# A block-sparse attention and SoLU kernel: the first pass rearranged and the order of the last two tiles changed

## The chip, the core and the metric

The kernel runs on one core of a Trainium2 chip. The core has a matrix engine (TensorE, PE in the profile; its weight loads are listed as PEld), VectorE (DVE), ScalarE (ACT), GpSimd (POOL) and SyncE (SP, which here only issues transfers). Each engine works through its own instructions in order and waits on semaphores for the others. Data moves between main memory and the on-chip SBUF by DMA, issued from the queues of SP, ACT or POOL; TensorE writes to PSUM, which has eight banks, and VectorE and ScalarE read it. The metric is device time in microseconds: a median of several runs, and one further execution taken with the hardware profiler.

## What is computed

Four sequences of 768 tokens have eight heads of 64 columns. Attention is masked in blocks of 32 by 32: a query block sees its neighbours, the first and last block, three drawn blocks per row, and everything if it is itself first or last. The result, as 3072 rows of 512, passes through a feed-forward layer whose activation is h times softmax(h), then a layer norm and a second matrix:

```python
scores = scale * np.matmul(q, k.transpose(0, 1, 3, 2))
scores = np.where(mask, scores, -1000000000.0)
attn = softmax(scores)
x = (attn @ v).transpose(0, 2, 1, 3).reshape(3072, 512)
h = x @ w_in                      # 512 -> 1024
solu = h * softmax(h)
ln = (solu - mean) / np.sqrt(var + 1e-06) * g_ln
out = ln @ w_out                  # 1024 -> 512
```

## The kernel before

**Tiling.** Heads go in pairs (NPR = 4 pairs), a head in each half of the 128 partitions. Keys are cut into six tiles of 128; one unit takes a pair, two key tiles (j of NJ = 3) and 256 queries (r of PPB = 3). So UP = 12 units make a pass, three passes a batch, and 144 units the whole attention. Unit s has a score (`score`, L327: four matmuls, L335), an exponential by ScalarE of 128x1024 (L348), a mask, and eight matmuls with v (`outs`, L365, L375). After three units VectorE divides by the row sums (`normalise`, L381).

**Masks.** Most units are masked by VectorE, which multiplies the exponentials with a 0/1 tile from `mask_sb` (`mask`, L355). For units with j = 1 after the first three, `adds_mask` (L350) has TensorE add a large negative number instead, by four further matmuls with `hid` and `onehot` (L343). Seven mask tiles are needed; `make_mask` (L548) builds them, two to a PSUM tile, by matmuls from `vis_t` and `onehot` and a copy.

**Turning k and q.** Both need the head's columns on the partitions. For batch 0 they are loaded as fp32, cast to bf16 (`cast_st`, L299, on VectorE), turned by six TensorE transposes into PSUM and copied out (`turn_kq`, L307; k by ScalarE, q by VectorE). For the other batches GpSimd casts and SP issues transposing DMAs (`turn_dma`, L315). v is only cast (`cast_v`, L304): by ScalarE in batch 0, by GpSimd later.

**Setup.** VectorE and GpSimd build the block mask (`vis`, L503 to L540) from the drawn blocks `samp_i`, which are loaded first on SP's queue (L488). k and q of pair 0 are loaded by SP and ACT, the other raw tiles, g_ln and w_out by SP. `onehot` and `hid` are copied to partitions 64 to 127 by DMAs from ACT's queue (L566). w_in comes by a GpSimd DMA (L576). Eleven matmuls on zeros (`N_IDLE`, L498) run first on TensorE.

**The second layer.** Each pass gives two tiles of 128 rows (t = 0 to 23). A tile goes through: transposing DMA (`moe_x`), h (`moe_h`), exponential, solu on VectorE (`moe_u`), transposing DMA (`moe_t`), statistics (`moe_b`, bn_stats twice), the reciprocal deviation by Ln and Exp on ScalarE (`moe_r`), eight matmuls with w_out (`moe_o`, L443), and scaling and storing (`moe_y`, L453). The last two tiles, 22 and 23, take functions of their own (`tail_x`, `tail_h`, `tail_e`, `tail_u`, `tail_t`, `tail_b`, L632 to L681), which turn by TensorE instead of DMA and work in halves. `check_r`, `check_e` and `check_b` test the range of all sums; the result `bad_i` is read by every engine at the end and decides whether a general path runs (it does not here).

**Order.** The order on each engine is that of the program: the loop (L725) runs slots s = 0, 1, 2, ...; in a slot come score(s), outs of older units, normalise, mask(s - 2), and then whatever `at(slot, ...)` has put down for it. Slot 147 (`s0 = n_units + LAG`) is the first after attention. An engine starts an instruction when the ones ahead of it in its own order and the data it needs are done, so slots set order, not times. DMAs issued from SP and ACT take turns on eight semaphores, and one waits until the earlier DMA on its semaphore has landed.

**PSUM.** `p_s` has three tiles of two banks (scores, h, masks, transposes), `p_op` one bank (P·V, and some of the last outputs), `p_o` one bank (outputs of the second layer, the eleven first matmuls, the mean of w_out).

Of the kernel before, what the change touches and what calls it, by code (L numbers as in the profile page):

```python
# [7 lines left out]
FP32 = mybir.dt.float32  # L8
# [193 lines left out]
def kernel(  # L202
# [11 lines left out]
    nc = tc.nc  # L214
# [92 lines left out]
    def turn_kq(which, b, a, copy):  # L307
        st = staged.pop((which, b, a)).rearrange("p i h d -> p i (h d)")
        tp = p_s.tile([TQ, NT, TQ], BF16, tag="s", name=f"tp{which}{b}_{a}")
        for i in range(NT):  # L310
            nc.tensor.matmul(tp[:, i, :], st[:, i, :], ident, is_transpose=True,
                             start=(i == 0), stop=(i == NT - 1))
        copy(out=(kTs, qTs)[which][b][:, a, :], in_=tp.rearrange("p i x -> p (i x)"))  # L313
# [36 lines left out]
    def adds_mask(s):  # L350


        return s >= NJ and s % NJ == 1
# [99 lines left out]
    def moe_y(t):  # L453
        ot = mo.tile([128, d_model], FP32, tag="ot", name=f"ot{t}")
        if t < n_tail - 2:
# [25 lines left out]
    def centre_w(c):  # L481
# [6 lines left out]
    nc.sync.dma_start(out=samp_i.rearrange("a b c -> a (b c)"),  # L488
                      in_=bass.AP(tensor=_t32, offset=0, ap=[[2 * NR, NB], [1, 2 * NR]]))
# [3 lines left out]

    idle = setup.tile([128, 512], BF16, name="idle")
    nc.vector.memset(idle, 0.0)
    idle_ps = p_o.tile([128, 512], FP32, tag="o")
    for i in range(N_IDLE):
        nc.tensor.matmul(idle_ps, idle[:, 0:128], idle, start=True, stop=True)  # L498
    nc.vector.memset(ident, 0.0)
    nc.gpsimd.affine_select(out=ident, in_=ident, compare_op=ALU.not_equal, fill=1.0,  # L500
                            base=0, channel_multiplier=1, pattern=[[-1, 128]])

    vis = setup.tile([NB, NB], FP32, name="vis")  # L503
    nc.vector.memset(vis, 1.0)
    onehot = setup.tile([128, NT, TQ], BF16, name="onehot")
    nc.vector.memset(onehot[0:64], 1.0)
    kbi = setup.tile([NB, NB], I32, name="kbi")
    nc.gpsimd.iota(kbi, pattern=[[1, NB]], base=0, channel_multiplier=0)
    for fill, base, cm, step in (
        (0.0, 1, -1, 1), (0.0, 1, 1, -1),  # L510
        (1.0, -1, 1, 0), (1.0, NB - 2, -1, 0),
        (1.0, -1, 0, 1), (1.0, NB - 2, 0, -1),
    ):
        nc.gpsimd.affine_select(out=vis, in_=vis, compare_op=ALU.is_ge, fill=fill,
                                base=base, channel_multiplier=cm, pattern=[[step, NB]])

    for base, cm, sgn in ((0, -BLK, 1), (BLK - 1, BLK, -1)):
        nc.gpsimd.affine_select(out=onehot[0:64], in_=onehot[0:64], compare_op=ALU.is_ge, fill=0.0,
                                base=base, channel_multiplier=cm,
                                pattern=[[sgn, NT], [sgn * NT, TQ]])  # L520
# [6 lines left out]
    for i in range(2):  # L527
# [3 lines left out]
                "(c p) m -> p c m", p=128))  # L531
    kbf = setup.tile([NB, NB], FP32, name="kbf")
    nc.vector.tensor_copy(out=kbf, in_=kbi)
    samp_f = setup.tile([NB, NR], FP32, name="samp_f")
    nc.vector.tensor_copy(out=samp_f, in_=samp_i[:, :, 0])
    for i in range(NR):
        nc.vector.scalar_tensor_tensor(out=vis, in0=kbf, scalar=samp_f[:, i : i + 1], in1=vis,
                                       op0=ALU.is_equal, op1=ALU.max)
    vis_t = setup.tile([NB, NB, BLK], BF16, name="vis_t")
    nc.vector.tensor_copy(out=vis_t, in_=vis.rearrange("p (q o) -> p q o", o=1)  # L540
                          .broadcast_to([NB, NB, BLK]))
    vis_k = vis_t.rearrange("a n o -> a (n o)").rearrange("a (p i) -> a i p", i=NT)

    mask_at = [(0, 0), (0, 1), (0, 2)] + [(r, j) for r in range(1, PPB) for j in (0, NJ - 1)]
    mask_sb = setup.tile([TQ, len(mask_at), 512], BF16, name="mask_sb")
    n_mask = (len(mask_at) + 1) // 2

    def make_mask(n, copy):  # L548
        m = p_s.tile([TQ, 2, 512], FP32, tag="s", name=f"m{n}")
        lst = mask_at[2 * n : 2 * n + 2]  # L550
        for u, (r, j) in enumerate(lst):
            for i in range(2):
                nc.tensor.matmul(m[:, u, i * 256 : (i + 1) * 256], vis_k[:, 2 * j + i, :],  # L553
                                 onehot[0:NB, r * QW : (r + 1) * QW, :],
                                 start=(i == 0), stop=(i == 1), skip_group_check=True)
        copy(out=mask_sb[:, 2 * n : 2 * n + len(lst), :], in_=m[:, 0 : len(lst), :])


    hid = setup.tile([128, S], BF16, name="hid")
    nc.gpsimd.memset(hid[0:64], 0.0)  # L560
    hid_k = hid.rearrange("a (p i) -> a i p", i=NT)
# [10 lines left out]
    for vb in vbuf:  # L572
        nc.vector.memset(vb[:, :, :, :, D:D1], 1.0)
    nc.vector.memset(mean_w, 1.0 / d_ff)
    nc.vector.memset(ones_c, 1.0)
    nc.gpsimd.dma_start(out=w_in_sb, in_=moe_w_in.rearrange("(c p) f -> p c f", p=128))  # L576
# [205 lines left out]
```

## Time and profile before

| | |
|---|---|
| median of 3 runs | 241.1 us (241.05 to 241.48) |
| profiled execution | 240.45 us, of which the span of the core 238.9 us |
| mean granted TensorE clock | 0.954 |
| busy: PE, DVE, ACT, POOL | 211.5, 195.4, 182.4, 38.7 us |
| first score starts | 10.28 us |
| last matmul of the second layer ends | 229.16 us |
| last ScalarE instruction ends | 233.29 us |

The profile lists busy time, but an engine that is busy need not set the end. The chain of work goes back from the last instruction, step by step, to what released it. The waits say for each engine what ended its idle time. Windows give busy time and the granted clock of any stretch. Times are microseconds from the start of the span, and L with a number is a line of the kernel.

### The profile page before, as it was taken

The page shows a single profiled execution, that of the slowest core. Times are in us where ns is not written, and L with a number is a line of the kernel's source. Part 1 is how long each engine was busy: PE and PEld are TensorE (multiplying, and loading weights), DVE is VectorE, ACT ScalarE, POOL GpSimd, SP SyncE. Part 2 cuts the span into 40 slices and gives each one's busy share as a digit, 9 for nine tenths or more (in the row PEclk, how much of TensorE's full clock was granted, in tenths as well). Part 3 has the DMA queues.
Part 4 walks back from the last instruction along what each step waited for, and adds up shares of the span by engine and source line. Part 5 has one row for each costly group of instructions (what it writes and reads, how often), then busy time and mean ns, then how long its engine had stood idle before and what let it go on. Part 6 is the DMA issues. An engine that isn't in the chain of part 4 may idle for free.

```text
span 238.9 us, 6023 instructions
## 1 busy us (share of the span) xinstructions
PE 211.5 (89%) x2407; PEld 109.9 (46%) x2407; DVE 195.4 (82%) x417; ACT 182.4 (76%) x263; POOL 38.7 (16%) x53
## 2 busy tenths in 40 slices
PE   7588877869999999998999997999999999999930
PEld 2265553544545444453454544445454545454410
DVE  6587679799898978888899889689988988896480
ACT  2496897967987888797798887889888988883630
POOL 6300030413122132411202132312000000000000
PEclk9755899999999999999999999999999999999996
DMA  6999917699999999999878999998832514333211
GB/s 191 340 265 316 365 29 150 149 227 199 261 179 230 202 190 276 230 184 218 223 166 204 196 214 258 209 206 224 130 74 59 134 44 86 92 91 88 84 42 62
DMA packets 73765, 42.33 MB, mean 177 GB/s; under 512 B 56708, under 2 KB 69124, under 8 KB 73732
## 3 DMA queue, kind: packets, MB, share of 16 engines
q1 hardware_dynamic: 72772, 40.26, 73.4%
q0 software_dynamic: 528, 1.05, 2.3%
q10 hardware_dynamic: 432, 0.59, 0.8%
q8 instruction: 20, 0.33, 0.6%
q14 instruction: 13, 0.11, 0.2%
HBM read 23.07 MB, written 6.29 MB: 123 GB/s over the span
## 4 chain that ended last, share of the span: by engine, by line
PE 50%; DMA 19%; DVE 14%; ACT 5%; issue 5%; SPq 4%; POOL 1%; ACTq 0%; POOLq 0%
PE o L450 12%; PE s L335 11%; PE h L406 10%; PE op L375 10%; DMA lnT<-solu 9%; DMA raw<-in_k_dram 5%; DVE ex L360 4%; ACT ex L348 3%; DMA raw<-in_q_dram 3%; SPq L317 2%; PE s L343 2%; DVE stats L426 2%; DMA raw<-in_v_dram 2%; DVE w_out_sb L482 2%; PE h L649 2%
## 5 line engine op out<-in xcount | busy, mean ns | idle before, releaser
L348 ACT ACTIVATE ex<-s 128x1024 bf16<-128x1024 f32 x144 | 139.0, 1023 | 6.8 <-PE s L335 5.3
L360 DVE TENSOR_TENSOR ex<-ex,mask_sb 128x1024 bf16<-128x1024 bf16 x97 | 70.2, 724 | 8.0 <-ACT ex L348 7.9
L335 PE MATMUL s<-qT,kT 64*128 64x256 bf16 x576 | 57.5, 282 | 4.7 <-DVE qT L313 1.9
L375 PE MATMUL op<-v,ex 128*128 128x65 bf16 x1152 | 52.9, 196 | 5.7 <-DVE ex L360 3.5
L450 PE MATMUL o<-w_out_sb,lnT 128*128 128x512 bf16 x192 | 52.0, 381 | 4.1 <-DMA lnT<-solu 3.2
L375 PEld LDWEIGHTS <-ex 128*128 128x128 bf16 x1152 | 41.4, 99 | 26.0 <-issue 13.1
L410 ACT ACTIVATE e<-h 128x1024 bf16<-128x1024 f32 x22 | 22.5, 1024 | 25.0 <-PE h L406 25.0
L406 PE MATMUL h<-w_in_sb,xT 128*128 128x512 bf16 x176 | 41.6, 379 | 0.0
L335 PEld LDWEIGHTS <-kT 64*128 64x128 bf16 x576 | 19.4, 95 | 42.9 <-issue 36.9
L301 POOL CAST st<-raw 128x768 bf16<-128x768 f32 x24 | 21.9, 911 | 82.8 <-DMA raw<-in_k_dram 56.0
L426 DVE BATCH_NORM_STATS2 stats<-solu 128x6 f32<-128x512 bf16 x44 | 30.0, 684 | 0.0
L415 DVE TENSOR_TENSOR solu<-h,e 128x1024 bf16<-128x1024 f32 x22 | 26.8, 1217 | 0.0
L450 PEld LDWEIGHTS <-lnT 128*128 128x128 bf16 x192 | 14.0, 97 | 21.3 <-issue 8.0
L456 DVE TENSOR_SCALAR ot<-o,rstd 128x512 f32<-128x512 f32 x20 | 15.0, 750 | 10.3 <-PE o L450 10.2
L406 PEld LDWEIGHTS <-xT 128*128 128x128 bf16 x176 | 15.9, 98 | 16.0
L389 DVE TENSOR_TENSOR xb<-op,recip_all 128x256 bf16<-128x256 f32 x48 | 20.4, 424 | 1.6
L343 PE MATMUL s<-onehot,hid 64*128 64x256 bf16 x188 | 18.6, 275 | 0.0
L305 POOL CAST v<-raw 128x768 bf16<-128x768 f32 x12 | 10.9, 905 | 43.4 <-DMA raw<-in_v_dram 37.4
L343 PEld LDWEIGHTS <-hid 64*128 64x128 bf16 x188 | 11.3, 123 | 0.6
L387 DVE RECIPROCAL recip_all<-op 128x4 f32<-128x4 f32 x48 | 8.4, 175 | 2.1 <-PE op L375 2.1
L313 ACT COPY kT<-tp 128x768 bf16<-128x768 bf16 x4 | 3.2, 806 | 7.2 <-PE m L553 7.2
L439 ACT ACTIVATE lnv<-vpe 128x1 f32<-128x1 f32 x24 | 4.9, 204 | 3.8 <-DVE vpe L434 3.8
(74 smaller groups left out, 106.5 us busy)
## 6 DMA issues: line engine op xcount, KB each, us to landing
raw<-in_k_dram SPq DMA_DIRECT2D x16, 384.0 KB, 4.6
raw<-in_v_dram SPq DMA_DIRECT2D x16, 384.0 KB, 4.0
out_dram<-ot SPq DMA_DIRECT2D x24, 256.0 KB, 3.7
raw<-in_q_dram SPq DMA_DIRECT2D x15, 384.0 KB, 5.1
w_out_f<-in_moe_w_out_dram SPq DMA_DIRECT2D x2, 1024.0 KB, 9.9
w_in_sb<-in_moe_w_in_dram POOLq DMA_DIRECT2D x1, 1024.0 KB, 13.3
raw<-in_q_dram ACTq DMA_DIRECT2D x1, 384.0 KB, 3.2
xT<-xb SPq DMA_TRANSPOSE x22, 3.1
```

What stands on the lines that cost most here:

```text
L301: copy(out=st.rearrange("p i h d -> p h i d"), in_=staged[which, b, a])
L335: nc.tensor.matmul(ps[:, par, n * 256 : (n + 1) * 256], kTs[b][lo : lo + 64, a, i * TQ : (i + 1) * TQ], qTs[b][lo : lo + 64, a, r * 256 : ...
L343: nc.tensor.matmul(ps[:, par, n * 256 : (n + 1) * 256], hid_k[lo : lo + 64, 2 * j + n, :], onehot[lo : lo + 64, r * QW : (r + 1) * QW, :], ...
L348: nc.scalar.activation(out=exs[s], in_=ps, func=ACT.Exp, scale=scale)
L360: nc.vector.tensor_tensor(out=exs[s], in0=exs[s], in1=mask_sb[:, m : m + 1, :].broadcast_to([TQ, 2, 512]), op=ALU.mult)
L375: nc.tensor.matmul(op[:, par * QW + c, :], ex[:, par, lo : lo + TQ], vbuf[b % 2][:, a, par, 2 * j + n, :], start=(j == 0 and n + par + c = ...
L389: nc.vector.tensor_tensor(out=dst, in0=op[:, :, 0:D].rearrange("p (h c) d -> p h c d", h=2), in1=recip.rearrange("p (h c) o -> p h c o", h ...
L406: nc.tensor.matmul(hs[t][:, half, :], xTs[t][:, c, :], w_in_sb[:, c, half * HF : (half + 1) * HF], start=(c == 0), stop=(c == KD - 1))
L410: nc.scalar.activation(out=es_of[t], in_=hs[t].rearrange("p a b -> p (a b)"), func=ACT.Exp, scale=1.0, accum_out=esum_all[:, t : t + 1])
L415: nc.vector.tensor_mul(out=solus[t], in0=hs.pop(t).rearrange("p a b -> p (a b)"), in1=es_of.pop(t))
L426: nc.vector.bn_stats(out=stats_of[t][:, i, :], in_=so)
L450: nc.tensor.matmul(o_ps[t], lnT, w_out_sb[:, f, :], start=(f == 0), stop=(f == KF - 1))
```

## The change

At the start:

- `samp_i` is loaded on ACT's queue, behind q of pair 0. All raw loads are written down before the rest of the setup.
- `hid` is zeroed by VectorE instead of GpSimd; `vis_t` is made by GpSimd instead of VectorE. The ones and constants are set ahead of the block mask's last steps.
- The upper halves of `onehot` and `hid` are copied by DMAs from GpSimd's queue instead of ACT's.
- w_in is loaded by GpSimd in slot 4, behind the casts of v for pairs 0 and 1.
- q of pair 0 is cast by ScalarE. k and q of batch 0 are turned through the single bank `p_o` (q of pair 0 through `p_s`), one slot earlier than before, and both are copied by VectorE.
- v of batch 0 is cast by GpSimd.
- Masks are made one to a PSUM tile of one bank, all copied by ScalarE: three by slot 0, the others in slots 8, 10, 14 and 17.
- In the first pass the masks of units 6, 7, 9 and 10 are added by TensorE (before: 4, 7, 10).
- Batch 1's loads begin in slot 14 instead of 10 and follow each other every 9/4 slots instead of 10/4.

At the end:

- Tile 19's output is scaled by ScalarE instead of VectorE.
- u of tile 23 follows u of tile 22 on VectorE. Tile 22's transposes come ahead of tile 21's output matmuls on TensorE, and all four copies of the turned halves go to ScalarE.
- Statistics of 22 and 23 follow on VectorE, ahead of the checks.
- Tile 23's output is made in two halves of 256 columns, in two PSUM tiles, scaled by ScalarE and stored from SP's and ACT's queues. The matmul of the check comes last on TensorE.

```diff
@@ turning
-    def turn_kq(which, b, a, copy):
+    def turn_kq(which, b, a, copy, pl=p_o, tag="o"):
         st = staged.pop((which, b, a)).rearrange("p i h d -> p i (h d)")
-        tp = p_s.tile([TQ, NT, TQ], BF16, tag="s", name=f"tp{which}{b}_{a}")
+        tp = pl.tile([TQ, NT, TQ], BF16, tag=tag, name=f"tp{which}{b}_{a}")
@@ masks added by TensorE
-        return s >= NJ and s % NJ == 1
+        return s >= 2 * NJ and (s % NJ == 1 or s < UP and s % NJ == 0)
@@ moe_y
-        if t < n_tail - 2:
+        if t < n_tail - 3:
@@ setup
-    nc.sync.dma_start(out=samp_i.rearrange("a b c -> a (b c)"),
-                      in_=bass.AP(tensor=_t32, offset=0, ap=[[2 * NR, NB], [1, 2 * NR]]))
     alloc_kq(0)
     load_raw(0, 0, 0, nc.sync)
     load_raw(1, 0, 0, nc.scalar)
+    nc.scalar.dma_start(out=samp_i.rearrange("a b c -> a (b c)"),
+                        in_=bass.AP(tensor=_t32, offset=0, ap=[[2 * NR, NB], [1, 2 * NR]]))
...
-    nc.vector.tensor_copy(out=vis_t, in_=vis.rearrange("p (q o) -> p q o", o=1)
+    nc.gpsimd.tensor_copy(out=vis_t, in_=vis.rearrange("p (q o) -> p q o", o=1)
...
-    nc.gpsimd.memset(hid[0:64], 0.0)
+    nc.vector.memset(hid[0:64], 0.0)
...
     for t in (onehot, hid):
-        nc.scalar.dma_start(out=t[64:128], in_=t[0:64])
-
-    for which in range(2):
-        cast_st(which, 0, 0, nc.vector.tensor_copy)
-        turn_kq(which, 0, 0, (nc.scalar.copy, nc.vector.tensor_copy)[which])
-    make_mask(0, nc.scalar.copy)
...
-    nc.gpsimd.dma_start(out=w_in_sb, in_=moe_w_in.rearrange("(c p) f -> p c f", p=128))
+        nc.gpsimd.dma_start(out=t[64:128], in_=t[0:64])
...
+    def make_mask(u, copy, pl=p_o, tag="o"):
+        m = pl.tile([TQ, 512], FP32, tag=tag, name=f"m{u}")
+        r, j = mask_at[u]
+        for i in range(2):
+            nc.tensor.matmul(m[:, i * 256 : (i + 1) * 256], vis_k[:, 2 * j + i, :],
+                             onehot[0:NB, r * QW : (r + 1) * QW, :],
+                             start=(i == 0), stop=(i == 1), skip_group_check=True)
+        copy(out=mask_sb[:, u, :], in_=m)
...
+    cast_st(0, 0, 0, nc.vector.tensor_copy)
+    cast_st(1, 0, 0, nc.scalar.copy)
+    turn_kq(0, 0, 0, nc.vector.tensor_copy)
+    turn_kq(1, 0, 0, nc.vector.tensor_copy, p_s, "s")
+    make_mask(0, nc.scalar.copy, p_op, "op")
+    make_mask(1, nc.scalar.copy, p_s, "s")
+    cast_st(0, 0, 1, nc.vector.tensor_copy)
@@ slots
     for a in range(NPR):
         for which in range(2 if a else 0):
-            at(3 * a - 3 + which, cast_st, which, 0, a, nc.vector.tensor_copy)
-            at(3 * a - 2 + which, turn_kq, which, 0, a,
-               (nc.scalar.copy, nc.vector.tensor_copy)[which])
-        at(3 * a + 1, cast_v, 0, a, nc.scalar.copy)
-    for n in range(1, n_mask):
-        at((0, 4, 7)[n - 1], make_mask, n, nc.vector.tensor_copy)
+            if a > 1 or which:
+                at(3 * a - 4 + which, cast_st, which, 0, a, nc.vector.tensor_copy)
+            at(3 * a - 3 + which, turn_kq, which, 0, a, nc.vector.tensor_copy)
+        at(3 * a + 1, cast_v, 0, a, nc.gpsimd.tensor_copy)
+    at(4, load_w_in)
+    at(0, make_mask, 2, nc.scalar.copy, p_op, "op")
+    for u, sl in enumerate((8, 10, 14, 17)):
+        at(sl, make_mask, u + 3, nc.scalar.copy)
...
-        s0 = (b - 1) * UP * PPB + (10 if b == 1 else 5)
+        s0 = (b - 1) * UP * PPB + (14 if b == 1 else 5)
...
-                sl = s0 + (3 * a + which) * 5 // 2
+                sl = s0 + (3 * a + which) * (9 if b == 1 else 10) // 4
@@ end
+    def last_oy(t):
+        for n, (pl, tag) in enumerate(((p_op, "op"), (p_s, "s"))):
+            cs = slice(n * d_model // 2, (n + 1) * d_model // 2)
+            o = pl.tile([128, d_model // 2], FP32, tag=tag, name=f"o{t}_{n}")
+            for f in range(KF):
+                nc.tensor.matmul(o, lnTs[t][f * 2 // KF][:, f % (KF // 2), :], w_out_sb[:, f, cs],
+                                 start=(f == 0), stop=(f == KF - 1))
+            ot = mo.tile([128, d_model // 2], FP32, tag=f"ot{n}", name=f"ot{t}_{n}")
+            nc.scalar.activation(out=ot, in_=o, func=ACT.Copy, scale=rstds[t])
+            b, i = t // NT, t % NT
+            (nc.sync, nc.scalar)[n].dma_start(
+                out=out[b * S : (b + 1) * S, cs].rearrange("(p i) m -> p i m", i=NT)[:, i], in_=ot)
...
-        (0, moe_o, (t0 - 1, 0, KF)), (0, tail_t, (t0, 0, nc.scalar.copy)),
-        (0, tail_t, (t0, 1, nc.vector.tensor_copy)), (0, moe_r, (t0 - 1,)),
-        (1, tail_u, (t1, 0)), (1, tail_u, (t1, 1)), (1, moe_y, (t0 - 1,)),
-        (1, moe_o, (t0, 0, KF)), (1, tail_t, (t1, 0, nc.scalar.copy)),
-        (1, tail_t, (t1, 1, nc.vector.tensor_copy)), (1, check_r, ()), (1, check_e, ()),
-        (2, moe_o, (t1, 0, KF)), (2, tail_b, (t0,)), (2, moe_r, (t0,)), (2, moe_y, (t0,)),
-        (2, tail_b, (t1,)), (2, check_b, ()), (2, moe_r, (t1,)), (2, moe_y, (t1,)),
+        (0, tail_t, (t0, 0, nc.scalar.copy)), (0, tail_t, (t0, 1, nc.scalar.copy)),
+        (0, moe_r, (t0 - 1,)), (0, tail_u, (t1, 0)), (0, tail_u, (t1, 1)),
+        (0, moe_o, (t0 - 1, 0, KF)), (0, tail_t, (t1, 0, nc.scalar.copy)),
+        (0, tail_t, (t1, 1, nc.scalar.copy)),
+        (1, moe_y, (t0 - 1,)), (1, tail_b, (t0,)), (1, moe_r, (t0,)), (1, moe_o, (t0, 0, KF)),
+        (1, tail_b, (t1,)), (1, moe_r, (t1,)), (1, moe_y, (t0,)), (1, check_r, ()),
+        (1, check_e, ()), (1, last_oy, (t1,)), (1, check_b, ()),
```

More of the change, by code (lines that the diff above doesn't have):

```diff
@@ L492 @@
     load_raw(1, 0, 0, nc.scalar)
[L494 to L520, printed above, removed]
+    nc.scalar.dma_start(out=samp_i.rearrange("a b c -> a (b c)"),
+                        in_=bass.AP(tensor=_t32, offset=0, ap=[[2 * NR, NB], [1, 2 * NR]]))
     for a in range(1, NPR):
```

55 lines of the change are left out of this document (37 added, 18 removed).

## The prediction

> **What bounds the kernel now.** I read the page first (busy shares, clock row), then the waits, then the start and the end of the trace as chain, windows and timeline.
>
> ```profile
> PE 211.5 (89%) x2407; PEld 109.9 (46%) x2407; DVE 195.4 (82%) x417; ACT 182.4 (76%) x263; POOL 38.7 (16%) x53
> PEclk9755899999999999999999999999999999999996
> ```
>
> TensorE is the busiest engine, yet the change touches only two places where it is not simply full: slices 2 to 5 of the clock row (about 6 to 26 us) and the last 20 us. The middle, where PE is busy 38.75 of 40 us in the windows from 60 to 100, keeps its instructions apart from batch 1's loads.
>
> The windows put edges on the slow stretch: the granted clock falls in the first and returns in the second.
>
> ```profile
> 8.80:9.00 0.20, 0.11 (x2) 0.00 (x0) 0.14 (x1) 0.00 (x0) 0.00 (x0) 0.69 1.07 399
> 25.80:26.00 0.20, 0.20 (x7) 0.20 (x6) 0.20 (x2) 0.11 (x1) 0.00 (x0) 0.64 1.08 399
> ```
>
> The second-last number is the clock: half speed from 8.9 to 25.9 us, most of the first pass. In that time four scores cost 0.54 us, eight P·V matmuls 0.50, six transposes about 0.7, four mask adds 0.43; at full clock 0.32, 0.35, 0.46, 0.22.
>
> The waits from 10 to 30 us, and those of the whole run:
>
> ```profile
> DVE mask_sb L556 <- PE m L553: 5.6, 3, 2.0
> PE s L335 <- DVE qT L313: 1.9, 3, 0.7
> ACT kT L313 <- PE m L553: 7.2, 1, 7.2
> ```
>
> PE stands three times before scores because qT of the next head pair is copied too late. The 7.2 us of ACT are misnamed: the transposes of k ended at 7.24, but ACT's queue held the copy of hid, issued only at 8.91; kT's copy began at 9.42 and the first score at 10.28.
>
> The end, from the chain:
>
> ```profile
> 226.84 0.42 DVE lnT L672
> 227.27 0.18 DVE okr L693
> ...
> 228.61 1.21 DVE stats L426 x2
> ...
> 230.39 1.21 DVE stats L426 x2
> ...
> 232.37 0.21 ACT rstd L441
> ...
> 232.60 0.69 ACT ot L459
> ```
>
> The chain runs on VectorE: copy, checks, statistics of tiles 22 and 23 one after the other, then tile 23's scale and output. PE's last output matmuls end at 229.16, four microseconds before ACT's end at 233.29.
>
> **The end.** Unchanged until VectorE starts u22 at 221.01 (moving tile 19's 0.74 us scaling from VectorE to idle ACT clears statistics, not u22, which waits for ACT's e). By the rows: u22 1.29 to 222.30, u23 right behind 1.28 to 223.58 (before, it began at 224.38, behind a copy), statistics 22 and 23 at 1.78 each to 227.14. PE: u22's transposes 0.46 to 222.76, o21 1.73 to 224.5, u23's transposes to 224.95, o22 1.9 to 226.85. ACT then sets the end: two copies of 0.59 from 224.95 to 226.15, ot21 0.69, Ln and Exp of 22 and 23 0.9, ot22 0.69 to 228.45. The two halves of tile 23 are 128x256; the nearest row is the 0.37 us copy of that width, the other bound the 0.69 of 128x512. I take 0.45 each: 229.35, and 0.3 for a dozen hand-overs of 0.02 to 0.05: 229.65. Against 233.29 that is **-3.65**. Behind ACT's last half its own store issue is queued, beside SP's, instead of one at 233.35; the wait for landing (2.8 us) I leave as it is. The 1.3 us of checks now lie on VectorE from 227.1 to 228.5 beside ACT, their result ready near 229.3, before the store lands; without that cover it would cost up to 1.3. The 16 half-wide matmuls could cost PE as much as 512-wide ones (16 at 0.216 after 226.85, so 230.3), which makes the gain -2.5; without hand-overs and with quicker small stores it is -4.3.
>
> **The first score.** samp_i leaves the head of SP's queue (k's load starts 0.49 earlier) for ACT's, behind q's 384 KB. Bounds: 1.4 us after its issue, as on SP before, so near 2.9; or behind the bulk, as the 4 KB of g_ln took 11.7 us behind other loads. q landed 3.2 us after 0.97 and now shares with k from the start; I take 4.9, the queue row being nearer. VectorE waits there in order, with k's cast and everything else behind it: 0.16 and three steps of 0.67 end at 7.1 (before 5.42). vis_t (0.76) and q's cast have left VectorE, so k's cast follows: 0.55, or 1.18 when GpSimd reads at the same time:
>
> ```profile
> L301 DVE CAST st<-raw x8: 534/552/1175, 6.1 to 23.1; 128x768 bf16<-128x768 f32 x8
> L360 DVE TENSOR_TENSOR ex<-ex,mask_sb x4: 681/788/1199, 27.7 to 32.2; 128x1024 bf16<-128x1024 bf16 x4
> ```
>
> The maxima fall where GpSimd worked (hid at 6.40 to 7.37, its cast at 31.80 to 32.85). Then transposes 0.51, kT copy 0.56 beside q's transposes, qT copy 0.56: first score near 9.45, against 10.28: -0.8. Ends: -2.4 (samp at 2.9) and +0.8 (samp at 6, cast locked).
>
> [...]
>
> **The rest of the first pass.** Turning one slot earlier removes PE's three waits, -1.9. The bank of its own stops masks and transposes from displacing scores. Three of five mask builds go past score 8, where they run later at about half the price (-0.6 of what I can place). Units 6 and 9 take an add on PE and unit 4 loses one, +0.43, while VectorE saves one mask. VectorE loses 3.14 of mask copies and gains 2.24 of kT copies. Four v casts leave ACT (0.83 each) for GpSimd (0.84); each can lengthen a VectorE operation by 0.5 to 0.6, half of them on the path: +1.0; the cover is POOL's idle, 16% busy. Two small copies (nearest issue row 0.91) go ahead of v0's cast on POOL: hid near 9.1, copies issued by 10.9, landed 6.4 later at 17.3; unit 6 needs them near 18.9. w_in moves from 7.4 behind v1's cast near 13 to 15; with 13.3 us it lands before 30, its first reader is at 39.2; and the raw loads lose a competitor. Sum to unit 9: -1.1, and -0.2 for the loads: -1.3. Bounds +1.2 (both late) and -3.
>
> From unit 9 to 20 ACT was full (exponentials back to back, 30.22 to 39.63), and there masks 4 to 6 at 0.59 replace v3's 0.84: **+0.9**. The front is thus -0.8 -1.3 +0.9 = **-1.2** at unit 20. Behind that PE and VectorE run full, in the same order, so it is carried.
>
> **Batch 1's loads four slots later.** On SP they pass xT's and output stores. Before, qT of pair 3 was issued at 71.38 and took 3.4 (74.8), and unit 45 needed it at 75.55: 0.75 of slack. Now k3's transpose (1.24) and tile 1's store (0.42) come between xT and it: 1.85 later with gaps, 1.1 us short at PE; a later wait for lnT at 79.07 (0.56) takes part of that. I book **+0.8**, bounds 0 and +2.5 (every one of batch 1's late transposes short).
>
> **Sum.** -3.65 -1.2 +0.8 = -4.05. The profiled execution took 240.45 (span 238.9 and about 1.6 around), so 236.4; the shown median lies 0.65 above it: **237.0**.
>
> **Rivals.**
> *GpSimd's queue holds the first pass.* [...] Chance 0.22.
>
> *Clock back early.* If PE's denser first pass brings full clock at 19 to 22.5, three units cost VectorE's 4.2 us (masks 1.4, normalise 0.6, casts 1.1, copies 1.1) instead of PE's 5.0 at half clock (scores 1.6, P·V 1.5, transposes 1.4, adds 0.43): over some four units -1.1; with the late transpose covered too, 235.1. Against: VectorE's casts still hold PE between units. Chance 0.14.
>
> *Clock stays low (the other side).* The place is the first pass and what follows: if gaps on PE keep half clock past 25.9, each further microsecond costs about 0.35 (1.25 us of PE a unit against ACT's 0.95), and 0.5 once MoE matmuls fill PE. It decides when half clock lasts until about 37, 11 us more: then 241 or over; I put 241.9. For: the drop is there, five slices long; against: units get closer together. Chance 0.07.
>
> [...]
>
> *Batch 1 starves.* SP is late for several pairs, 2.5 instead of 0.8, or 4: 238.7 to 240.5, rarely beyond 241.6. Chance 0.10.
>
> *As forecast,* 235.8 to 238.2: chance 0.47.
>
> **Numbers.** 0.2% of 241.1 is 0.5 us, about what a measurement can tell. Forecast, GpSimd case and early clock hold 0.83, starving below 240.6 adds 0.05, and 0.03 goes off for an end that does not come: faster 0.85. Starving near 241 gives same 0.03; low clock 0.07, the far end of starving 0.02 and the failed end 0.03 give slower 0.12. The range 234.0 to 239.7 takes in the bounds of the end and the first score and leaves about 0.05 below and 0.15 above.
>
> **What would show it.** End: u23 directly behind u22, ACT's last half near 229.6 less the front's shift, the chain's tail on ACT in place of VectorE's statistics. Start: samp_f near 4.9, first score near 9.5, no PE wait for qT. Unit 20's exponential near 38.4. A PE wait of about 1 us for qT near unit 45. Wrong: a clock row with half speed past slice 5, PE waiting for hid's copy, or PE as the last engine at the end.

## The result and the profile after

The changed kernel took 235.0 us (median; 233.15 to 235.51) against 241.29 (241.05 to 243.11) for the kernel before on the same chip: ratio 0.9709, interval 0.9638 to 0.978. Its profiled execution took 234.99 us, span 233.39; before, 240.45 and 238.85. So 5.46 us left the span. Executions of one kernel differ by 0.6 to 6.0 us (the ranges in the table of experiments). A profile is one such execution, so stages are compared below, and times only with their intervals. Ratios compare means and leave out executions more than 1.5% above the fastest of the same kernel, so they are not always the quotient of the two medians.

From the records of both traces, four stretches make the 5.46 us:

| stretch | before | after | difference |
|---|---|---|---|
| start to the end of the last exponential | 214.28 | 212.78 | -1.50 |
| to the start of tile 22's u on VectorE | 6.73 | 6.74 | +0.01 |
| to the end of ScalarE's last scaling | 12.28 | 7.90 | -4.38 |
| to the end of the span | 5.56 | 5.97 | +0.41 |

The page's busy shares and clock row of the changed kernel (40 slices, the clock in tenths):

```profile
PE 211.2 (91%) x2419; PEld 109.5 (47%) x2419; DVE 190.0 (81%) x413; ACT 181.4 (78%) x266; POOL 44.6 (19%) x59
PEclk9659997999999999999999999999999999999997
```

TensorE's work is what it was; the span is shorter around it. The slow slices are now 2 and 3, and slice 7 is new. The windows (busy time of each engine, then clock, DMA share and GB/s) give the edges:

```profile
18.10:18.30 0.20, 0.20 (x4) 0.07 (x3) 0.20 (x2) 0.00 (x0) 0.20 (x1) 0.52 1.04 266
18.30:18.50 0.20, 0.20 (x10) 0.20 (x8) 0.20 (x2) 0.15 (x1) 0.20 (x1) 1.00 0.94 225
31.95:35.36 3.41, 1.62 (x30) 1.01 (x27) 3.38 (x9) 3.41 (x5) 0.00 (x0) 1.00 0.76 174
36.00:37.00 1.00, 1.00 (x7) 0.45 (x5) 1.00 (x3) 0.58 (x1) 1.00 (x1) 0.50 1.22 243
```

Full speed is back at 18.3 us instead of 25.9. From 35.36 to 38.77 it is half again, after a stretch in which TensorE (the first busy time) was busy 1.62 of 3.41 us.

TensorE's waits from 10 to 30 us are two lines now:

```profile
PE tp L311 <- DVE st L301: 1.3, 3, 0.5
PE op L375 <- DVE ex L360: 0.3, 1, 0.3
```

The three waits of scores for qT (1.9 us) are gone; what TensorE still waits for, 1.6 us, is VectorE's casts of k and q and one mask. The windows from 13 to 24 us, of the kernel before:

```profile
13.00:24.00 11.00, 9.68 (x97) 6.61 (x96) 8.23 (x16) 8.90 (x11) 0.00 (x0) 0.50 1.10 291
```

and of the changed kernel:

```profile
13.00:24.00 11.00, 9.55 (x127) 6.05 (x126) 10.35 (x20) 7.59 (x10) 2.39 (x3) 0.76 1.10 275
```

VectorE (third) is busy for 10.35 of 11 us instead of 8.23, and ScalarE (fourth) for 7.59 instead of 8.90.

The end, from the chain (start, duration, what):

```profile
217.58 1.04 PE h L656 x4
...
219.52 2.48 DVE u L670 x4
...
222.07 1.21 DVE stats L426 x2
...
223.85 1.21 DVE stats L426 x2
...
225.40 0.17 DVE vpe L434
225.57 0.02 issue
225.60 0.21 ACT lnv L439
...
226.51 0.91 ACT ot L719 x2
```

The copies and checks have left VectorE's chain; both u and both statistics stand in a row, and only then comes ScalarE.

How far ahead of the kernel before the exponential of each unit ends (one profiled execution each, us; negative is earlier). This is the lead below, and "unit 11 ended" means its exponential:

| unit | 0 | 4 | 6 | 9 | 11 | 18 | 20 | 24 | 45 | 48 | 60 | 96 | 143 |
|---|---|---|---|---|---|---|---|---|---|---|---|---|---|
| after | -0.65 | -0.58 | -3.04 | -3.67 | -3.90 | -2.92 | -3.05 | -1.80 | -2.26 | -0.94 | -0.33 | -1.45 | -1.49 |

### The profile page after: what moved, and what is told of

The parts are those of the page before. It is cut to its first block, busy times and chain, and to the rows that moved or that the text cites. A ratio compares the mean times of both kernels' runs of the same rounds, so it can differ in the third digit from the quotient of the medians.

```text
span 233.4 us, 6054 instructions
## 1 busy us (share of the span) xinstructions
PE 211.2 (91%) x2419; PEld 109.5 (47%) x2419; DVE 190.0 (81%) x413; ACT 181.4 (78%) x266; POOL 44.6 (19%) x59
## 3 DMA queue, kind: packets, MB, share of 16 engines
q0 software_dynamic: 624, 1.25, 2.7%
## 4 chain that ended last, share of the span: by engine, by line
PE 60%; DVE 15%; DMA 13%; ACT 4%; issue 3%; SPq 1%; POOL 0%; POOLq 0%; DVEq 0%; ACTq 0%
PE o L450 14%; PE h L406 13%; PE s L335 13%; PE op L375 12%; DMA lnT<-solu 9%; DVE ex L360 4%; PE s L343 3%; ACT ex L348 3%; DMA raw<-in_k_dram 2%; DVE stats L426 2%; DMA samp_i<-in_sampled_blocks_dram 2%; PE tp L311 2%; PE h L656 2%; DVE w_out_sb L482 1%; DVE w_out_sb L471 1%
## 5 line engine op out<-in xcount | busy, mean ns | idle before, releaser
L360 DVE TENSOR_TENSOR ex<-ex,mask_sb 128x1024 bf16<-128x1024 bf16 x96 | 68.9, 718 | 9.2 <-ACT ex L348 9.1
L450 PE MATMUL o<-w_out_sb,lnT 128*128 128x512 bf16 x184 | 50.3, 381 | 3.9 <-DMA lnT<-solu 3.9
L406 PE MATMUL h<-w_in_sb,xT 128*128 128x512 bf16 x176 | 42.9, 388 | 0.0
L301 POOL CAST st<-raw 128x768 bf16<-128x768 f32 x24 | 22.8, 951 | 82.2 <-DMA raw<-in_k_dram 48.1
L335 PEld LDWEIGHTS <-kT 64*128 64x128 bf16 x576 | 18.5, 94 | 40.4 <-issue 35.9
L456 DVE TENSOR_SCALAR ot<-o,rstd 128x512 f32<-128x512 f32 x19 | 14.3, 750 | 10.8 <-PE o L450 10.8
L450 PEld LDWEIGHTS <-lnT 128*128 128x128 bf16 x184 | 13.3, 97 | 19.9 <-issue 8.0
L305 POOL CAST v<-raw 128x768 bf16<-128x768 f32 x16 | 14.6, 911 | 34.8 <-DMA raw<-in_v_dram 26.0
L311 PE MATMUL tp<-ident,st 128*128 128x128 bf16 x48 | 5.5, 276 | 3.5 <-DVE st L301 3.5
L570 ACT CAST mask_sb<-m 128x512 bf16<-128x512 f32 x7 | 4.3, 624 | 3.2 <-PE m L567 3.2
```

What stands on the lines that cost most here:

```text
L301: copy(out=st.rearrange("p i h d -> p h i d"), in_=staged[which, b, a])
L335: nc.tensor.matmul(ps[:, par, n * 256 : (n + 1) * 256], kTs[b][lo : lo + 64, a, i * TQ : (i + 1) * TQ], qTs[b][lo : lo + 64, a, r * 256 : ...
L360: nc.vector.tensor_tensor(out=exs[s], in0=exs[s], in1=mask_sb[:, m : m + 1, :].broadcast_to([TQ, 2, 512]), op=ALU.mult)
L406: nc.tensor.matmul(hs[t][:, half, :], xTs[t][:, c, :], w_in_sb[:, c, half * HF : (half + 1) * HF], start=(c == 0), stop=(c == KD - 1))
L450: nc.tensor.matmul(o_ps[t], lnT, w_out_sb[:, f, :], start=(f == 0), stop=(f == KF - 1))
```

## The experiments

All are the changed kernel with one thing altered, unless said otherwise. Ratios are against the kernel before on the same chip at the same time (median 241.29 us for the changed kernel, then 243.16 for the first four runs, 241.81 for the next four, 242.75 for the last four):

| run | median us (lowest to highest) | ratio (interval) | unit 11 to unit 11 of the changed kernel |
|---|---|---|---|
| changed kernel | 235.0 (233.15 to 235.51) | 0.9709 (0.9638 to 0.978) | 0 |
| new end alone | 240.01 (239.59 to 242.91) | 0.9885 (0.9791 to 0.9979) | |
| old end | 239.13 (237.87 to 240.71) | 0.9802 (0.9719 to 0.9884) | +1.03 |
| batch 1's loads as before | 235.72 (233.5 to 236.73) | 0.9648 (0.9562 to 0.9735) | -0.02 |
| 21 first matmuls | 238.82 (237.25 to 239.03) | 0.9788 (0.9714 to 0.9861) | -0.05 |
| samp_i on SP | 235.39 (231.26 to 237.23) | none taken | -1.14 |
| matmuls in slot 18 | 238.47 (237.85 to 238.48) | 0.9848 (0.9787 to 0.9909) | +0.73 |
| v cast by ScalarE | 234.13 (233.42 to 235.5) | 0.9667 (0.9606 to 0.9728) | +0.76 |
| turned in score tiles | 236.74 (233.03 to 238.59) | 0.9686 (0.958 to 0.9793) | +0.18 |
| masks in old slots | 233.65 (232.68 to 235.43) | 0.9663 (0.9563 to 0.9764) | +0.94 |
| turned a slot later | 236.79 (235.72 to 238.17) | 0.9781 (0.9685 to 0.9878) | +0.35 |
| last output in one piece | 236.4 (235.77 to 239.75) | 0.9769 (0.9698 to 0.984) | -0.13 |
| samp_i on SP, v by ScalarE | 239.57 (237.58 to 241.3) | 0.9879 (0.9775 to 0.9982) | +2.82 |

### The end alone, and the front alone

The first puts the new order of the end into the kernel before, the second puts the old end back:

```diff
-    (0, moe_o, (t0 - 1, 0, KF)), (0, tail_t, (t0, 0, nc.scalar.copy)),
+    (0, tail_t, (t0, 0, nc.scalar.copy)), (0, tail_t, (t0, 1, nc.scalar.copy)),
...
-    (2, tail_b, (t1,)), (2, check_b, ()), (2, moe_r, (t1,)), (2, moe_y, (t1,)),
+    (1, check_e, ()), (1, last_oy, (t1,)), (1, check_b, ()),
```

> The kernel before, with the new end alone (tile 19 on ScalarE, u of both tiles in a row, statistics ahead of the checks, last output in halves). Theory A, the two parts of the change are independent and the end is worth what its own instructions show: the stretch from the last second-layer input matmul to the end of the span shrinks by 4.0 us (18.75 before, 14.8 after) and the time falls by 3.7 to 4.2, to about 237.2. Rival B, the end only gains because the front hands it its data earlier: under 2.5 us. First score and the clock's slow stretch stay as before (first score near 10.3, half clock 17 us or a neighbouring multiple of 3.4).

> The changed kernel with the old end. Theory A: the start alone gives the rest, 1.0 to 2.5 us, so 238.6 to 240.1, and the lead over before is 3 to 4 us at unit 11, but at most 2.3 from unit 45 on, because it is given back in the middle. Rival B, the start gains nothing that arrives: within 0.5 of before (241). Its runs should differ among each other by more than those of before, following the mean clock of each run (about 0.7 us for 0.01 of mean clock).

From the start of u22 to ScalarE's last scaling the end took 7.90 us with the new order, in whichever kernel it stood, and 12.28 with the old one, in both kernels that have it. (The run with one last output, below, is the exception.) So the end's 4.38 us up to there do not depend on the front, and rival B falls. The time of the new end alone fell by 3.15 us, less than the 3.7 to 4.2 expected; its interval reaches from 0.5 to 5.1. In its profile, with two stretches of half clock at 50.0 and 80.7 us, unit 143 ended 4.14 later than in the kernel before, ahead of nearly all that the new end touches. The two ratios multiplied, 0.9885 times 0.9802, give 0.969, against 0.9709 for the whole change: as far as the intervals tell, the two parts add. The front alone was worth 1.2 to 2.8% of 243.16, 2.8 to 6.8 us, more than the 1.50 us that the profiles show. Its lead in its own profile was 2.87 at unit 11 and 1.93 at unit 45; at unit 48 it was 0.66 behind, with half clock from 79.0 to 82.4. Its executions did not follow their mean clock, as was expected of them: 240.36 at 0.963, 237.87 at 0.954.

### Batch 1's loads

```diff
-        s0 = (b - 1) * UP * PPB + (14 if b == 1 else 5)
+        s0 = (b - 1) * UP * PPB + (10 if b == 1 else 5)
...
-                sl = s0 + (3 * a + which) * (9 if b == 1 else 10) // 4
+                sl = s0 + (3 * a + which) * 5 // 2
```

> The changed kernel, but batch 1's loads in slots 10 and following, every 10/4, as before. Theory A, the later loads cost TensorE little (0.3 us waiting for qT in the profile): time within 0.6 of the changed kernel, 234.4 to 235.6, and no wait of TensorE for qT near unit 45. Rival C, my booked 0.8: the old slots are 0.8 faster, near 234.2, with the lead at unit 48 grown by as much. Rival D, the later start of the loads is what lets the transposing DMAs of the middle land: the old slots are slower by 0.5 or more.

The intervals overlap nearly whole (0.9562 to 0.9735 and 0.9638 to 0.978). A cost of 0.8 us for the later loads is not seen in the times, nor a gain. In the profile TensorE no longer waits for qT from 40 to 100 us, and unit 48 ended 1.29 earlier than in the changed kernel, as rival C asked; at unit 60 nothing of that was left (0.01).

### The clock in the first pass

```diff
-    N_IDLE = 11
+    N_IDLE = 21
```

> The changed kernel with 21 instead of 11 matmuls on zeros ahead of the first transposes (10 more at 0.216 us, from 5.5 to about 7.7, when k's cast is ready). Theory E, the first pass is slow because the clock falls for want of work on TensorE between 5.5 and 8.7: the half-clock stretch of 10.2 us starts later or does not come, unit 11's exponential ends 1 to 2.5 us earlier, and the time falls by 0.5 to 1.5. Rival F, VectorE's casts and copies and ScalarE bound the first pass in any case: unit 11 within 0.5 of the changed kernel, time the same within 0.5. If the fills end after k's cast the first score moves by the overlap, at most 0.3 later.

The clock row says what ten more matmuls on zeros did:

```profile
PEclk9979997999999799999999999999979999999996
```

In the first pass half speed shrank to one stretch, 14.48 to 17.89. Unit 0 ended 0.56 earlier than in the changed kernel, unit 3 1.0 earlier, and unit 11 only 0.05. VectorE's work is where the lead went. In the timelines of the two kernels (start, duration, idle time before in brackets) it reaches the same reciprocal at the same time. The changed kernel first:

```profile
19.51 0.17 DVE L387 RECIPROCAL recip_all<-op 128x4 f32<-128x4 f32 x1
19.71 0.42 DVE L389 TENSOR_TENSOR xb<-op,recip_all 128x256 bf16<-128x256 f32 x1
```

And with 21 matmuls:

```profile
18.36 1.19 DVE L301 CAST st<-raw 128x768 bf16<-128x768 f32 x1
19.46 0.16 DVE L387 RECIPROCAL recip_all<-op 128x4 f32<-128x4 f32 x1
19.66 0.42 DVE L389 TENSOR_TENSOR xb<-op,recip_all 128x256 bf16<-128x256 f32 x1
```

Up to there three of VectorE's casts and masks took 0.95 to 1.19 us instead of 0.55 to 0.68 in the run with 21 matmuls, while in the changed kernel two masks took 1.31 and 0.84. That is about 0.5 us of the lead; the rest is not accounted for. Rival F is right about unit 11: full speed earlier than 18.3 us gained nothing there. It is not right about the time, 238.82: two more stretches of half clock, at 79.3 and 171.5 us, stand in this profile, and unit 143 ended 3.80 later than in the changed kernel. Whether the added matmuls brought them is not shown.

### Where the first pass was won

Five runs undo one part each:

```diff
@@ samp_i at the head of SP's queue
+    nc.sync.dma_start(out=samp_i.rearrange("a b c -> a (b c)"),
+                      in_=bass.AP(tensor=_t32, offset=0, ap=[[2 * NR, NB], [1, 2 * NR]]))
     alloc_kq(0)
...
-    nc.scalar.dma_start(out=samp_i.rearrange("a b c -> a (b c)"),
...
@@ v cast by ScalarE
-        at(3 * a + 1, cast_v, 0, a, nc.gpsimd.tensor_copy)
+        at(3 * a + 1, cast_v, 0, a, nc.scalar.copy)
@@ turned in score tiles
-    def turn_kq(which, b, a, copy, pl=p_o, tag="o"):
+    def turn_kq(which, b, a, copy, pl=p_s, tag="s"):
@@ turned a slot later
-            at(3 * a - 3 + which, turn_kq, which, 0, a, nc.vector.tensor_copy)
+            at(3 * a - 2 + which, turn_kq, which, 0, a, nc.vector.tensor_copy)
@@ masks in old slots
-    for u, sl in enumerate((8, 10, 14, 17)):
-        at(sl, make_mask, u + 3, nc.scalar.copy)
+    for u, sl in enumerate((4, 4, 7, 7)):
+        at(sl, make_mask, u + 3, nc.vector.tensor_copy, p_s, "s")
```

> The changed kernel, with samp_i back at the head of SP's queue and nothing else altered. Theory W: VectorE, which stands 2.84 us before the cast of samp_f at 6.10, holds the start of the changed kernel. Then samp_f runs near 3.9 to 4.3, the first score starts 0.7 to 1.2 us earlier than 9.74 (k's load begins 0.5 later, and k's cast follows it), and unit 0 ends that much earlier; as VectorE and ScalarE are full in the first pass, unit 11 ends 0.5 to 1.2 earlier too. Rival K: k's own load sets the first score, samp_i or not; then the first score moves by under 0.3 us or comes later. In both the middle takes part of it: the time changes by 0 to -1 us.

> The changed kernel with the four casts of batch 0's v on ScalarE again. Theory V: ScalarE's time in the first pass is what the move to GpSimd bought; four casts of 0.83 come back on an engine that also carries the seven mask copies, so unit 11 ends 2 to 3 us later than in the changed kernel, and the lead over the kernel before is 1 to 2 at unit 11. [...] Time: +1 to +2.5 by V if the lead is carried, within 0.6 by L.

> The changed kernel with k and q of batch 0 turned through the two-bank score tiles again, at the same slots. Theory T: the bank of its own is what removed TensorE's waits; transposes again hold a score tile until VectorE has copied it, so scores of the next units wait for tiles, TensorE's idle time in the first pass grows by 1.5 to 3 us and unit 11 ends 1 to 2.5 later. Rival S: the earlier slot did it, not the bank: unit 11 ends within 0.6 of the changed kernel. Time: +0.5 to +2 by T, within 0.5 by S.

> The changed kernel with the last four masks built in slots 4, 4, 7 and 7 through the score tiles and copied by VectorE, as in the kernel before, though each by itself. Theory M: taking these builds out of the first pass (two of 1.03 us on TensorE at half clock, two copies of 1.2 on VectorE) is the main part of the lead of 3.9 us at unit 11, 2.4 of which arise between units 4 and 6. Then unit 6 ends 1 to 2.5 later than in the changed kernel (20.28), unit 11 ends 2 to 3.5 later, and units 12 to 20 win back 0.5 to 1.5 as ScalarE has three copies less. Rival N: the earlier turning is the main part; then unit 11 is within 1 us of the changed kernel. Time: +0.5 to +2 by M, if the middle hands part of it on, within 0.8 by N.

> The changed kernel with k and q of pairs 1 to 3 turned one slot later, as in the kernel before; the casts stay. Theory N: turning earlier is what took TensorE's waits for qT away; the three waits come back (before: 1.9 us in all), and unit 11 ends 1.5 to 3 us later than in the changed kernel. Theory M (the masks are the main part): the waits come back in part and unit 11 ends 0.3 to 1.5 later. Time: +0.5 to +1.5 by N, under 1 by M.

*samp_i on SP.* The first score began at 8.31 instead of 9.74 and unit 0 ended 1.49 earlier, more than theory W gave; unit 11 kept 1.14. VectorE's wait for samp_i does hold the start. VectorE's three small steps took 1.98 us here, beside GpSimd's selects again, instead of 0.77. In the times nothing of it can be told (235.39, from 231.26 to 237.23).

*v by ScalarE.* Unit 10 ended 0.04 later and unit 11 0.76: near rival L (casts on GpSimd cost VectorE what they save ScalarE, and unit 11 moves by under 0.7) at first, a little over its bound at the end, and far from theory V's 2 to 3. What GpSimd's casts cost shows in VectorE's masks. The groups from 2 to 30 us (count, busy, mean ns, idle before), of the changed kernel:

```profile
L360 DVE TENSOR_TENSOR ex<-ex,mask_sb 128x1024 bf16<-128x1024 bf16 x9 | 7.0, 773 | 1.1 <-ACT ex L348 1.1
L301 DVE CAST st<-raw 128x768 bf16<-128x768 f32 x7 | 3.8, 549 | 0.0
```

With v on ScalarE:

```profile
L360 DVE TENSOR_TENSOR ex<-ex,mask_sb 128x1024 bf16<-128x1024 bf16 x9 | 6.2, 686 | 1.9 <-ACT ex L348 1.8
L301 DVE CAST st<-raw 128x768 bf16<-128x768 f32 x7 | 3.8, 550 | 0.0
```

Nine masks cost 0.8 us more beside GpSimd's casts, and VectorE's own casts nothing in these two executions. VectorE then waits 0.8 longer for exponentials, so the two evened out.

*The bank.* Turning through score tiles moved unit 11 by 0.18, and TensorE's waits hardly grew (1.9 instead of 1.6 us): theory T is not borne out. *The slot.* Turning one slot later brought waits back:

```profile
PE s L335 <- DVE qT L313: 1.3, 2, 0.7
PE m L567 <- DVE qT L313: 0.7, 1, 0.7
```

That is 2.0 us of TensorE's time, but the 1.3 us of waits for casts are no longer there, so its waits grew from 1.6 to 2.3 in all. Unit 11 moved by 0.35: theory N is not borne out either. *The masks.* Built early by VectorE they made unit 8 1.87 later and unit 11 0.94, below theory M's 2 to 3.5; by unit 18 all was won back (-0.04), since ScalarE has three copies less there. The timeline shows the price on VectorE:

```profile
17.85 1.29 DVE L570 CAST mask_sb<-m 128x512 bf16<-128x512 f32 x2
```

No single part carries the 3.9 us. The masks moved unit 11 by 0.94, v by 0.76, the slot by 0.35, the bank by 0.18, but these sizes are not safe. Four other runs have the changed kernel's own code up to unit 11, and there it ended 1.03 later (old end), 0.73 later (matmuls in slot 18), 0.02 earlier (loads as before) and 0.13 earlier (last output in one piece). In the two late ones half clock lasted to 21.0 and 21.2 us, in the others to 18.3 (the changed kernel), 19.0 and 19.8. Unit 0 lay between 0.70 earlier and 0.27 later in these four, so the 1.49 of samp_i stand out. With the masks in old slots it lasted to 23.2, so those 0.94 can be the clock's. What is shown is the front as a whole: unit 11 ended 2.87 to 4.03 ahead of the kernel before in all five executions with this code. Copies of k on VectorE, q's cast on ScalarE and the adds of units 6 and 9 were not tried alone. In the times the four of these runs that have an interval are not told apart from the changed kernel. The lowest median, 233.65 with masks in the old slots, is not told apart from 235.0 either: 0.9563 to 0.9764 against 0.9638 to 0.978. In its profile unit 143 ended 1.41 later than in the changed kernel; the 2.37 us that it won came behind ScalarE's last scaling, where a pause of VectorE is missing that is told of at the end.

### Half clock in the middle

```diff
-    for u, sl in enumerate((8, 10, 14, 17)):
+    for u, sl in enumerate((8, 10, 14, 16)):
...
+    at(18, fill, 5)
```

> The changed kernel with five matmuls on zeros put on TensorE in slot 18, ahead of score 19, and the last mask built in slot 16 instead of 17, so that the bank is free. They fill TensorE's two gaps from 32 to 34.2 us, which lie ahead of the stretch of half clock at 35.4 to 38.8. Theory G: the gaps bring that stretch. Then the clock stays full from about 18 to 70 us, the first eight h matmuls take 1.9 us instead of 3.25, and unit 24 ends about 1.2 us earlier than in the changed kernel, the lead at unit 24 staying near 3. Rival H: the stretch does not depend on these gaps; it is there again and unit 24 ends up to 0.6 later, by the price of the matmuls. For the end: if the lead is carried, the time falls by about 1.2 us; if the waits for lnT at units 45 to 60 set the pace whatever arrives earlier, it changes by under 0.5.

The windows of this run, beside those of the changed kernel above:

```profile
31.95:35.36 3.41, 2.40 (x26) 1.24 (x25) 3.38 (x10) 3.41 (x5) 0.00 (x0) 1.00 0.68 154
36.00:37.00 1.00, 1.00 (x16) 0.56 (x15) 1.00 (x3) 1.00 (x2) 0.65 (x1) 1.00 0.92 298
```

TensorE was busy 2.40 instead of 1.62 us and the clock stayed full; the first eight h matmuls took 1.89 us instead of 3.25. Unit 20 ended 0.93 later than in the changed kernel and unit 24 0.80 earlier, so the slow stretch cost 1.7. That agrees with theory G, though not as proof: with v on ScalarE the stretch was missing as well, without any filling, and unit 24 was 1.33 earlier. Nothing came of it: at unit 48 this run was 1.82 ahead of the changed kernel and at unit 60 0.69 behind. In between TensorE stood 1.0 us for xT, and up to 95.68 it stood 2.0 for lnT:

```profile
PE o L450 <- DMA lnT<-solu: 2.3, 2, 2.0
```

The changed kernel also waits for lnT (2.4 in two waits), 1.5 of it up to 78.12. Its chain shows that transfer, with the h matmuls of the slow stretch further up:

```profile
36.20 3.06 PE h L406 x8
...
72.72 5.36 DMA lnT<-solu
```

In the kernel before, the same transfer was released at 73.84 and landed at 79.02, and TensorE stood 0.6 us for it. The changed kernel released it 1.12 earlier and had it 0.94 earlier, though unit 45 had ended 2.26 earlier; about 1 us of the rest shows as the longer wait (1.5 instead of 0.6). The time of the run with the matmuls in slot 18 is worse than the changed kernel's: 0.9848, from 0.9787 to 0.9909, against 0.9638 to 0.978. Its first pass had half clock to 21.2, and another stretch came at 96.3; whether the matmuls brought them is not shown.

### The halves of the last output

```diff
-        (1, check_e, ()), (1, last_oy, (t1,)), (1, check_b, ()),
+        (1, check_e, ()), (1, moe_o, (t1, 0, KF)), (1, moe_y, (t1,)), (1, check_b, ()),
```

> The changed kernel with tile 23's output made as one tile of 512 columns, scaled in one piece by ScalarE and stored from one queue, in the same order of everything else. Theory P: the order (u of both tiles in a row, statistics ahead of the checks) made nearly all of the end's 4 us, and the halves little: the matmuls are done long before the statistics, so the halves only split the last scaling (0.91 in two, against 0.69 in one) and start a store 0.45 earlier. Then the stretch from the last h matmul of the tail to the end of the span changes by -0.3 to +0.4 from 14.77. Rival Q: two stores in two queues end sooner: +0.5 to +1.5.

From u22 to ScalarE's end it took 8.14 instead of 7.90, and from the last h matmul of the tail to the end of the span 14.55 (238.16 less 223.61) instead of 14.77. Theory P holds: the order made the end; the halves gave ScalarE 0.24, and the span nothing.

### Two parts together

```diff
+    nc.sync.dma_start(out=samp_i.rearrange("a b c -> a (b c)"),
...
+        at(3 * a + 1, cast_v, 0, a, nc.scalar.copy)
```

> A candidate for a faster version: the changed kernel with samp_i at the head of SP's queue and batch 0's v cast by ScalarE. In the two single runs the first of these brought unit 11 1.14 us forward and the second left it within 0.8 of the changed kernel with no loss of time. If both add up, the first score starts near 8.7 and unit 11 ends 0.4 to 1.2 before the changed kernel's 27.35. For the time: if the middle carries the lead, 0.5 to 1 below the changed kernel; if late landings of lnT and single stretches of half clock between 35 and 100 us decide, the same within 0.8, with a spread of 2 us or more from run to run.

They did not add up. Unit 0 was 2.26 earlier, unit 11 2.82 later, and the time 239.57. In its waits from 10 to 24 us VectorE stands for a raw tile of k, which it did in neither of the two single runs:

```profile
DVE st L301 <- DMA raw<-in_k_dram: 2.6, 1, 2.6
```

Half clock followed from 21.5 to 28.3. Why the load landed late was not found.

## Why the prediction was right, and where it was not

The forecast was 237.0 and the range 234.0 to 239.7; 235.0 lies in it, 2.0 below the likeliest value and outside the 235.8 to 238.2 of that case. Of these 2.0 us, 0.7 are the end, which gave 4.38 instead of 3.65, and 1.1 the front with the loads, 1.50 instead of 0.4. Another 0.65 are the step from profile to median: it was added because the kernel before had it, and the changed kernel's profiled execution was at its median. The landing took 0.4 back. The 1.1 rest on one execution each. Step by step, the kernel before being the measure (in the prediction's two lines of windows the clock is the third number from the end, 0.69 and 0.64, not the second; the edges read from them are right):

**The end, -3.65.** The mechanism was right; u23 stood right behind u22 and statistics ended at 225.57, which in the times of before is 227.06, against 227.14 worked out. ScalarE's last scaling came 4.38 earlier instead of 3.65. The mis-sized term is ScalarE's sum. It added whole durations and 0.3 for hand-overs, while in the trace the next instruction begins before the row of the last one ends: tile 21's scaling at 224.21 is listed with 0.70, and Ln follows at 224.79, 0.58 later. With that ScalarE had time to spare, and it is VectorE's statistics that set the end, contrary to "ACT then sets the end". Sixteen half-wide matmuls took 1.91 us, so that bound was not needed; a half took 0.455, as booked (0.45). The landing, left "as it is", did change, and is told below.

**The first score, -0.8.** It was 9.74 instead of 9.45, so -0.54. samp_f came at 6.10, even past the late bound of 6. Two terms on the other side were too large: the three small steps took 0.77 instead of 2.01, and k's cast was not lengthened (0.54). So qT's copy ended at 9.42, nearly as worked out. The score began 0.32 behind it, for a term that the sum did not have: TensorE was still at the two mask builds, 1.05 us from 8.76 at half clock. In the run with the loads as before they took 0.74, and the score followed qT's copy by 0.05. The groups of the kernel before and after:

```profile
L537 DVE SCALAR_TENSOR_TENSOR vis<-kbf,samp_f,vis 24x24 f32<-24x24 f32 x3 | 1.9, 645 | 1.0 <-POOL vis L514 0.9
```

```profile
L544 DVE SCALAR_TENSOR_TENSOR vis<-kbf,samp_f,vis 24x24 f32<-24x24 f32 x3 | 0.7, 231 | 0.2
```

Before, GpSimd worked beside them (1.78 us of selects from 3.35 on); after, it waited for their result. With samp_i on SP the selects ran beside them again, and they took 1.98 us.

**The rest of the first pass, -1.3.** From unit 0 to unit 9 it was -3.0, the end of the bounds. The step that failed is the sum itself: waits of TensorE, mask work, and the price of GpSimd's casts were added up one by one. The runs show that single parts undone give 0.2 to 0.9 each, within what executions of the same code differ; 2.0 us of returning waits took the place of 1.3 others and moved unit 11 by 0.35. That parts hide behind each other, and that VectorE's list of work then decides, fits its 10.35 busy of 11 us, but is not shown by a run: in the two executions with half clock to 21.0 and 21.2 us unit 11 ended 1.03 and 0.73 later as well. GpSimd's casts, booked at +1.0, cost VectorE 0.8. No run shows a lock, as in the prediction's "cast locked"; the rows show nine masks at 773 ns on average beside GpSimd's casts and at 686 without them (one took 1.31 us), VectorE's casts at 549 and 550, and the small steps at 645 beside GpSimd's selects and at 231 without them. The masks on ScalarE, +0.9, were right: the lead fell from 3.90 at unit 14 to 2.92 at unit 18.

**"Carried".** This failed in the profile: the lead of 3.05 at unit 20 was 1.49 at the end. A stretch of half clock at 35.4 took 1.25 between units 20 and 24, and the wait for lnT 1.3 between 45 and 48. The old end's run, the same code nearly up to unit 143, had 0.87 left there. By the times, however, the front alone was worth at least 2.8 us, so the net of -0.4 that was booked for front and loads together was too small.

**Batch 1, +0.8.** Not seen. TensorE's wait for qT there was 0.3 us, and undoing the loads changed no time.

**The rivals.** GpSimd's queue did not hold the first pass: its two DMA issues took 0.72 and 0.53 us, and no wait for hid appears. "Clock back early" met its condition, full speed at 18.3, and its 235.1 is nearly the time measured; yet its reason is only half borne out: making the clock full still earlier left unit 11 where it was, while two executions in which it came back near 21 us ended unit 11 0.7 and 1.0 later. That the time came near 235.1 is luck, since that sum has the end at 3.65. Clock staying low and batch 1 starving did not come.

## What to carry to other kernels

Where several waits are removed at once, do not add them: find the engine whose list of work is full afterwards, and compare its work before and after. Before putting a size on one part, see how far executions of the same code differ at that place; here it was as much as any part gave. An order at the end of a kernel, where nothing runs ahead, can be worked out from rows to within a microsecond, with the distance of starts rather than the listed durations; a lead at the front has to survive every transfer and clock change behind it, and its size can be read only from several executions.

## What was not expected of the hardware

*A pause after the branch.* The last data of the output had landed at 229.06 us in the changed kernel, 1.6 after the last issue; before, the one store of 256 KB took 3.7 (issue 233.35, last data 237.08). So the halves land 2.1 sooner. The size alone is not the reason: the other 256 KB stores of the last tiles landed in 2.0 to 2.4 us in these two kernels, and the reason was not found. But VectorE's branch on the check's result began at 228.29 and its next instruction came at 232.28, while the other engines went on within half a microsecond; the span ends 1.1 later. Every new-end run has this pause, 3.3 to 4.0 us, except the one with masks in the old slots (0.61), where the stretch from ScalarE's end to the span's end was 3.60 instead of 5.4 to 6.0. The kernel before and the one with the old end have 0.61. That run had four more copies on VectorE; what makes the pause was not found. In the changed kernel it hides the earlier landing of the halves.

*The clock's steps.* In all these profiles half speed lasted a multiple of 3.41 us wherever both its beginning and its end are on record (3.41, 6.83, 10.24, 13.65, 17.07): 17.07 in the kernel before, from 8.88, and 10.24 and 3.41 in the changed kernel, from 8.05 and 35.36. The stretch at 35.36 followed 3.41 us in which TensorE was busy for 1.62, its longest gap 1.09. The busy share alone does not separate the steps before a fall from the others: in the run with the loads as before a window with 1.72 busy (169.19 to 172.60) was followed by full speed, and with 21 first matmuls one with 1.79 (31.55 to 34.96) by half. But the overlap is narrow. Take each profile in steps of 3.41 us from one of its clock changes, and leave out the first 20 us and the last stretch, where work runs out. At full clock all 14 steps in which TensorE was busy under 1.65 us were followed by half, 8 of the 38 with 1.65 to 2.32, and none of the 757 with more.
